# Thresholded attention and max-out FFN on one core: two unscaled quads, 41 half tiles masked by GpSimd, product and out tiles evacuated by VectorE, a new order

## The chip, the cores and the metric

The kernel runs on one core of one Trainium2 chip. The metric is the device time of one execution in microseconds (us). Engines are named as in the profile: PE is TensorE (PEld its weight loads), DVE is VectorE, ACT is ScalarE, POOL is GpSimd, SP is SyncE, which here only issues DMAs.

## The reference

```python
def _attn_ref(q, k, v, tau):                 # (8, 8, 576, 64) each, tau 0.02
    scale = 1.0 / np.sqrt(q.shape[-1])
    scores = scale * np.matmul(q, k.transpose(0, 1, 3, 2))
    thresh = np.max(scores, axis=-1, keepdims=True) - tau
    scores = np.where(scores >= thresh, scores, -1000000000.0)
    scores = scores - np.max(scores, axis=-1, keepdims=True)
    attn = np.exp(scores)
    attn = attn / (np.sum(attn, axis=-1, keepdims=True) + 1e-09)
    return np.matmul(attn, v)

def _moe_ref(x, w1, w2, w3, w_out):          # x (4608, 512), d_ff 768
    h = np.maximum(np.maximum(x @ w1, x @ w2), x @ w3)
    return h @ w_out
```

The heads of the attention's output are put side by side (8 heads of 64 make 512 columns), and the 4608 rows go through the FFN.

## The kernel before, in words

**Tiles.** A quad is four heads of one batch; there are 16 quads (`g`), two a batch. The 576 rows of a head are nine chunks of 64, and a tile joins 128 query rows, so that a quad has nine steps (`idx` 0 to 8), each with two half tiles (`r` 0 and 1) of 128 rows by 576 keys: 16 x 9 x 2 = 288 half tiles. Step 4 joins rows of two heads.

**Path of a half tile.** `transposed` (line 293, letter T) turns q and k on PE; `evacuated` copies them out (a: q by ACT, c: k mostly by DVE); `swapped` (q) copies q to the other 64 partitions, nearly always on POOL. `scores` (324, S) multiplies in float32 into one of four PSUM slots. `maximum` (364, m) lets DVE write minus the scores to a z buffer in SBUF (or the scores less tau) and take the row extremum `nm`. What follows hangs on the half tile's digit in `MASKED` (line 24):

- 0: `threshold` (375, s) makes `th` on DVE; `exponents` (379, e) runs a Prelu on ACT that is flat where the score reaches the threshold; `numerators` (388, n) runs the exponential on ACT, which steeply sends all else to zero and sums the row.
- 2: the same, but Prelu reads the scores in PSUM and needs no s.
- 1: e is the exponential on ACT, and `numerators` (k) masks on DVE: one pass that compares with exp(-tau), multiplies and sums, with both inputs in SBUF.
- 3: as 1, but e reads the scores in PSUM.

Then `reciprocals` (396, r, DVE) inverts the two row sums of a step, `normalized` (400, p, POOL) scales each half of z into the bf16 tile P, and `turned` (409, t) issues one DMA transpose of P on SP's queue into `ptq`.

**Product and FFN.** When the nine steps of a quad are turned, `product` (415, O) multiplies with v: 20 matmuls for each r, of 512 and of 64 columns. The result is copied to `xt` in bf16 by DVE for r = 0 (w) and by ACT for r = 1 (x). When both quads of a batch are there, `ffn` (479) makes 18 hidden pieces (6 slices by 3 weights; F issues the first half of the matmuls, B the second), with ACT copying the first weight's result to `hm` (h) and DVE taking the maximum with the other two (v). The out pieces (also F and B, with `done` at 545) are copied to `ob` by ACT (u) and stored (o) by SP; the last piece is copied by DVE (f) and stored by ACT's queue (d). Row chunk 8 has its own piece (N, j, i). The last batch is split in two parts (`SPLIT`), to shorten the end.

**Order.** Every engine runs its instructions in the order of issue: `_Ordered` (84) chains each to the one before it on its engine. The order is the string `ORDER` (40), written out in the kernel: each letter issues the next instruction of its kind (`issue`, 719), and for S, T, O, F and N a digit names the PSUM slot. Further letters: l loads q, k and v by SP's queue, y casts v on POOL, g loads and z casts weights (POOL).

Of the kernel before, what the change touches and what calls it, by code (L numbers as in the profile page):

```python
# [15 lines left out]
OP = AluOpType  # L16
# [19 lines left out]
PBUFS = 6  # L36

SPLIT = {7: ((0, 1), (2, 3, 4))}

ORDER = """  # L40
lllllllllT0laqqlcT1aS2lcqqgmS0S3lemS1lmnT2lmeS3lsaS0mnqlqemT3lyerclcapsnS1lS2eqmlS3qemznmS2perS1mnpsmnpT3ske
ytS1erkpT2agmnT3pclesqS2aqetS0meqlrnspmS1eqsT2nmpS3tnrcS0zlemS2eprmS3npmtS0npsgS1sermpS2emyS3eptmT0eplmS1ayl
meS0kynS2tssT3snkynkercperlT3pmnpmntqremS0lasprgeT3pmeS2psstnplnS0mzecesqrmS3etqkeS2gpnmS1npsmtnS0prmleS3pmS
2npsmnS0yrsmetperS2epmO1eqtnkplemnzswT2teS3rplS1empnmS3tpnssrS1klepS0mapermtS2epmT1S3nmqtnkO2qemncpS3txrskT1
peS2rmeS0ptmegpamS2npS1ertsmpnlkzS2elmS3eS0mpnlO1srkepsmnO2tyeprgwnpmT1xS3cpeS0sszmF2eS1meBqkF0ngqT3shrsmBay
S2tvpnF3rpemS1BpemF0pnsvT2BnyctS1esrlsT2mphS3lezS1maF0myntpT2sS3ngrcqF1eBmpnS2svpBnrmS3peS0tmeyF2zmnF3lBsvep
S0rhkBptesF2mgeS1zvF0nsmBpteBsrgvpnF1kS3phS2semBnqmF0S3evqF2ntrmBpelS1spvBnlmS3qhF0rsmepS1tnBpsmS3ezvS2eS1rm
pF0etsyO3mnlkngpO2eswetkBxrmpT3nF2rvpaS1BnqmS0hspS3meF2prS1smntBzesmF3ezvT0tBeclT1yS2pnvS0apsmtS3eyrmlS1epS2
mepF0mnqsmnS3tkBnkeF1restpkumeS2prtBumlperkpS0ustS2umS3pesmS1eqtT0mO2nlpceqsrmO3ntywelkS0pxlS1meF3prnS2smBye
myF0thpskS1oeBpF2nlvF3nlrmBpeBkpS1hstsvS0eF3lrmpnF2mBepBsveF1nT0vBtarkS3lhqS2smleF0prF1mnBysntBveS2plvnS0pom  # L50
F3nyS1pmeBsysmF0thT2rrlpeS1clF3epsmBnqT2svBaS1evqS2nmF0pS3nmqBtnmT2pS1hrcpS3esmS0petF2melS1rmpBnF3skpetF0sve
# [53 lines left out]
def kernel(  # L105
# [79 lines left out]

    def load(g, first=False):
        b, qd = quads[g]
        L = Ls[g] = dict(b=b, qd=qd, first=first)

        for n in "qk":  # L190
            L[n] = ld.tile([128, 16, D], F32, name=n + "m")
# [638 lines left out]
```

## Time and profile before

| | before |
|---|---|
| median of 3 runs | 442.02 us (441.42 to 442.81) |
| span of the profiled execution | 440.2 us |
| PE busy | 418.9 us (95%) |
| ACT busy | 403.6 us (92%) |
| DVE busy | 393.9 us (89%) |
| POOL busy | 317.0 us (72%) |
| score matmul records / ph matmuls | 1280 / 2160 |

The span runs from the first to the last instruction; the runs' times lie around it and are a little longer. A row of a group of instructions reads: line, engine, operation, out<-in by the program's names, shapes, count | busy us, mean ns of one | idle time of the engine before them and what ended it. All rows carry line 93, that of the helper that records the order, so tiles are told apart by name: sc is a score tile, z (or stage, when a spare weight buffer serves as z) the working half tile, P the normalized one, ptq the turned one, o the product, ph the hidden and po the out piece in PSUM. A row of windows reads: the stretch, its length, then busy us and (in brackets) instructions of PE, PEld, DVE, ACT and POOL, the granted clock, the share of DMA and GB/s.

### The profile page before, as it was taken

What the parts mean: (1) busy time and instruction counts of PE and PEld (TensorE: products, weight loads), DVE (VectorE), ACT (ScalarE), POOL (GpSimd) and SP (SyncE); (2) the same over time, 40 slices, a digit from 0 to 9 for tenths busy, and PEclk for the clock granted to TensorE, in tenths of its full rate; (3) what the DMA queues carried; (4) which work ended last, traced back from release to release, by engine and by line L of the source; (5) the groups of instructions that cost most, each with busy time, mean ns of one, the idle gap of its engine ahead of it and who ended that gap; (6) DMA issues with size and microseconds to landing.
All of it is one profiled execution on the core that took longest, in us unless ns stands there. A gap on an engine that the chain in (4) does not pass through costs nothing.

```text
span 440.2 us, 14283 instructions
## 1 busy us (share of the span) xinstructions
PE 418.9 (95%) x5188; PEld 313.6 (71%) x5190; DVE 393.9 (89%) x1248; ACT 403.6 (92%) x834; POOL 317.0 (72%) x420
## 2 busy tenths in 40 slices
PE   7696789999999999999999999999999999999996
PEld 6353446787788776787678777887688777786873
DVE  4888899999999999999999999999889999998542
ACT  4999999999999999999999999999999998989521
POOL 1988999998787778867786778886585776554400
PEclk9987999999999999999999999999999999999999
DMA  6999999999999999999999999999698778583812
GB/s 190 276 239 214 270 215 260 263 252 252 220 277 224 237 165 242 291 160 232 189 242 238 202 182 273 192 199 208 135 237 153 147 109 185 102 169 72 192 50 85
DMA packets 213959, 88.50 MB, mean 201 GB/s; under 512 B 189184, under 2 KB 202240, under 8 KB 213888
## 3 DMA queue, kind: packets, MB, share of 16 engines
q1 hardware_dynamic: 213360, 86.96, 95.4%
q8 instruction: 41, 0.67, 0.6%
q10 hardware_dynamic: 528, 0.62, 0.5%
q14 instruction: 30, 0.25, 0.2%
HBM read 35.65 MB, written 9.44 MB: 102 GB/s over the span
## 4 chain that ended last, share of the span: by engine, by line
PE 78%; DVE 5%; POOL 5%; issue 4%; ACT 3%; DMA 2%; SPq 1%; DVEq 0%; POOLq 0%; ACTq 0%
PE ph L93 31%; PE sc L93 26%; PE po L93 10%; PE o L93 8%; POOL P L93 4%; PE tp L93 3%; ACT z L93 3%; DVE z L93 3%; DMA qm<-in_q_dram 2%; SPq L93 1%; DVE kt L93 1%; POOL w L93 1%; DVE stage L93 0%; DVE hm L93 0%; POOL qs L93 0%
## 5 line engine op out<-in xcount | busy, mean ns | idle before, releaser
L93 POOL TENSOR_SCALAR P<-z,rs 128x576 bf16<-128x576 f32 x250 | 202.0, 819 | 59.1 <-DVE rs L93 30.4
L93 DVE TENSOR_SCALAR_CACHE_REDUCE z<-sc 128x576 f32<-128x576 f32 x250 | 183.2, 749 | 12.2 <-PE sc L93 8.1
L93 PE MATMUL sc<-kt,qs 64*128 64x256 f32 (+2 forms) x640 | 179.8, 417 | 5.5 <-DVE z L93 3.9
L93 PE MATMUL sc<-kt,qt 64*128 64x320 f32 (+2 forms) x640 | 180.9, 429 | 3.1 <-DVE z L93 1.2
L93 PE MATMUL ph<-xt,w 64*128 64x288 bf16 (+2 forms) x2160 | 172.0, 283 | 0.2 <-DVE hm L93 0.2
L93 PEld LDWEIGHTS <-w 64*128 64x128 bf16 (+1 forms) x2160 | 128.0, 94 | 31.6 <-issue 4.0
L93 ACT ACTIVATE z<-z,th 128x576 f32<-128x576 f32 x161 | 120.5, 767 | 2.2 <-DVE th L93 1.9
L93 ACT ACTIVATE z<-z 128x576 f32<-128x576 f32 x175 | 117.6, 674 | 0.2
L93 PEld LDWEIGHTS sc<-kt,qs 64*128 64x128 f32 (+1 forms) x640 | 92.4, 179 | 22.5 <-DVE z L93 8.6
L93 PEld LDWEIGHTS sc<-kt,qt 64*128 64x128 f32 (+1 forms) x640 | 92.0, 179 | 14.7 <-DVE z L93 3.5
L93 DVE SCALAR_TENSOR_TENSOR z<-z 128x576 f32<-128x576 f32 x75 | 61.7, 827 | 1.4 <-ACT z L93 1.1
L93 POOL COPY qs<-qt 64x640 f32<-64x640 f32 (+3 forms) x66 | 45.9, 695 | 19.5 <-ACT qt L93 16.1
L93 ACT ACTIVATE z<-z,nm 128x576 f32<-128x576 f32 x72 | 53.9, 767 | 0.0
L93 PE MATMUL po<-wo,hT 64*128 64x512 bf16 (+3 forms) x454 | 53.3, 354 | 0.3
L93 DVE TENSOR_TENSOR hm<-ph,hm 128x576 bf16<-128x576 f32 (+2 forms) x54 | 37.0, 685 | 9.8 <-PE ph L93 9.6
L93 ACT ACTIVATE hm<-ph 128x576 bf16<-128x576 f32 (+2 forms) x54 | 31.9, 590 | 14.3 <-PE ph L93 13.8
L93 PEld LDWEIGHTS <-hT 64*128 64x128 bf16 (+2 forms) x456 | 28.4, 95 | 18.5 <-issue 2.6
L93 DVE TENSOR_TENSOR hT<-ph,hm 128x576 bf16<-128x576 f32 (+2 forms) x54 | 36.9, 683 | 2.8 <-PE ph L93 1.0
L93 PE MATMUL o<-ptq,vb 128*64 128x512 bf16 (+2 forms) x544 | 38.7, 282 | 0.2 <-DVE z L93 0.2
L93 POOL TENSOR_SCALAR P<-stage,rs 128x576 bf16<-128x576 f32 x38 | 29.5, 783 | 11.7 <-DVE rs L93 8.4
L93 ACT ACTIVATION_READ_ACCUMULATOR z<-z 128x1 f32 x175 | 33.6, 192 | 0.0
L93 PEld LDWEIGHTS <-vb 128*64 128x64 bf16 x544 | 22.4, 111 | 14.0 <-issue 5.6
(44 smaller groups left out, 412.2 us busy)
## 6 DMA issues: line engine op xcount, KB each, us to landing
vm<-in_v_dram SPq DMA_DIRECT2D x32, 256.0 KB, 4.6
qm<-in_q_dram SPq DMA_DIRECT2D x15, 512.0 KB, 4.7
km<-in_k_dram SPq DMA_DIRECT2D x15, 512.0 KB, 5.4
out_dram<-ob SPq DMA_DIRECT2D x14, 512.0 KB, 4.5
stage<-in_moe_w_dram SPq DMA_DIRECT2D x9, 512.0 KB, 5.6
ptq<-P SPq DMA_TRANSPOSE x144, 4.5
vr<-in_v_dram SPq DMA_DIRECT2D x16, 128.0 KB, 3.8
stage<-in_moe_w_out_dram SPq DMA_DIRECT2D x3, 512.0 KB, 5.5
```

What stands on the lines that cost most here:

```text
L93: ins = fn(*a, **kw)
```

## The change

**Unscaled quads.** For the quads 0 and 1 (`LOOSE = 2`: batch 0) numerators go straight to P in bf16 without a row sum; r and p fall away. The row sums come from PE: four further products (one for each quad and r) take a column of ones in place of v, broadcast to 64 columns. ACT takes their logarithm (L) into an `ob` buffer and then the exponential of its negative (E), which is one over the sum; when the real product is there, DVE multiplies the two (w). The table set with logarithm and exponential is loaded by name at the start.

**Digits 4 and 5.** For digit 4 (41 half tiles) POOL masks: b adds the threshold to z, multiplies by 2^100 and writes the result as saturated int8 into every second byte of a bf16 tile `far` (a score under the threshold leaves a huge number, any other one zero), C adds `far` to z, and G is ACT's one exponential. Digit 5 is digit 3 with the comparison made on the scores in PSUM against `th`. By digits the 288 half tiles go from 187 / 84 / 14 / 3 (digits 0 to 3) to 192 / 37 / 10 / 2 / 41 / 6 (digits 0 to 5).

**Evacuation.** All products go to DVE (w; no x is left), and the second of each pair of out tiles does too (f: 15 instead of 1, u: 17 instead of 31). Each out pair has its own `ob` tile, `hm` has two buffers instead of three.

**Order.** The string is new throughout. ONE_S, ONE_R and BY_DMA, which would join thresholds or reciprocals of two half tiles or let DMAs do the swaps, are set beyond the range in use and do nothing here. Of the two strings the first seven lines are shown; the diff is cut to its core.

```diff
 FLAT = 2.0 ** -100
 
 MASKED = """
-220202110002002100110000100020020312000112012010100000000010100000001100
-001000111010000101100000000000110001100000011110110200100000100010000000
-110001101110100100010000001001100100000100101111102300000100100000001000
-001000110100100001000000000100100001011110100011011100002100001000001013
+421201000404010544201014040421043014041450550100100000010000000000100001
+000000100050001400100010400000000140000000410000001422400000010000000044
+000040401002210000004000400004000000041000040010101000001004004000010000
+004000000100400100400004401000000400010000105104200040400004001040041032
 """
...
-SPLIT = {7: ((0, 1), (2, 3, 4))}
+FARS = 1
+ONE_S = 999
+ONE_R = 999
+LOOSE = 2
+X_ON_DVE = True
+U_ON_DVE = True
+BY_DMA = 99
+FAR = 2.0 ** 100
+SPLIT = {7: ((0, 1), (2, 3, 4),)}
 ORDER = """
-lllllllllT0laqqlcT1aS2lcqqgmS0S3lemS1lmnT2lmeS3lsaS0mnqlqemT3lyerclcapsnS1lS2eqmlS3qemznmS2perS1mnpsmnpT3ske
-ytS1erkpT2agmnT3pclesqS2aqetS0meqlrnspmS1eqsT2nmpS3tnrcS0zlemS2eprmS3npmtS0npsgS1sermpS2emyS3eptmT0eplmS1ayl
-meS0kynS2tssT3snkynkercperlT3pmnpmntqremS0lasprgeT3pmeS2psstnplnS0mzecesqrmS3etqkeS2gpnmS1npsmtnS0prmleS3pmS
-2npsmnS0yrsmetperS2epmO1eqtnkplemnzswT2teS3rplS1empnmS3tpnssrS1klepS0mapermtS2epmT1S3nmqtnkO2qemncpS3txrskT1
-peS2rmeS0ptmegpamS2npS1ertsmpnlkzS2elmS3eS0mpnlO1srkepsmnO2tyeprgwnpmT1xS3cpeS0sszmF2eS1meBqkF0ngqT3shrsmBay
-S2tvpnF3rpemS1BpemF0pnsvT2BnyctS1esrlsT2mphS3lezS1maF0myntpT2sS3ngrcqF1eBmpnS2svpBnrmS3peS0tmeyF2zmnF3lBsvep
-S0rhkBptesF2mgeS1zvF0nsmBpteBsrgvpnF1kS3phS2semBnqmF0S3evqF2ntrmBpelS1spvBnlmS3qhF0rsmepS1tnBpsmS3ezvS2eS1rm
...
+lllllllllT0laclqqT1S0alqqclmS1lS3mS2lS0melsmeS3blT1mnlCaclS0esmlqeS2mqlGT1ysS0mlalecqmtnqsykS1eyS3nmS2essS0m
+bnS1mnT3CsestmakS0eqT3T2cGlqasmS3tbnmS1eqS2mtnqsemCemT1T0tssS2cabsGS0mqeS1tmqekS0nClS2mnlmS1gysmT0etmT2Gbsnk
+S1CascS3etS2mbnS0kGyT1semCtemS3nmyS2qlessS0mbelsketCmGS3meS2tbmnS0cnCS3tGssmO1eymlGmS0lbLskegS1qntmeCmS0nS3s
+skS1ebS2metGmCS0nmT3ezsmaskyGO3smetbEkO1CngswtkLT3qcES2btS0GmS1eCmO3esrmzGtS1ewpnskgT3palrmS2plsrT1mepS3lezs
+mlnkpgesclS0qeS2rtkpnS3mnO1ymeprsmS0qeS2rspLmO3ezskEtO0pnmelpS2snwgS1qLmlO3yemtEsrysS0npwS2epmtS1eF3ympnBspF
+0mnBzhsT1evF3tS2akS0nrrF1mpetBpmeS2BprnvtS0pnmF3hqsrT2sgBeczF1evS2qgnsmBlepF3mtnpBssvS2pheT0mpS3aF1trspmnS2T
+0znBmS3ecpF2termF0pnBvplS3nsvqS1gesBmzeS2mhF3grnsS1smplS0nmqBleS2symtF1esrF0vpeBknpBveO3pmhtesS1rwpnS2mF0pel
...
 """
...
+                if i == 0 and LOOSE:
+                    scalar.preload_act_table_set("natural_log_exp_and_others")
...
+    def loose(g):
+
+        return g < LOOSE
+
     def masked(g, idx, r):
-        return by_mask[2 * number[g, idx] + r] in "13"
+        return by_mask[2 * number[g, idx] + r] in "135"
+
+    def on_pool(c, r):
+        return by_mask[2 * number[c["g"], c["idx"]] + r] == "4"
...
     def direct(c, r):
 
-        return by_mask[2 * number[c["g"], c["idx"]] + r] in "23"
+        return by_mask[2 * number[c["g"], c["idx"]] + r] in "235"
...
     def maximum(c, r):
 
         z = c["z", r] = half_of_z()
-        nm = c["nm", r] = small.tile([128, 1], F32, name="nm")
+        if r == 0:
+            c["nms"] = small.tile([128, 2], F32, name="nm")
+        nm = c["nm", r] = c["nms"][:, r:r + 1]
...
     def threshold(c, r):
-        th = c["th", r] = small.tile([128, 1], F32, name="th", bufs=5)
-        vector.tensor_scalar(out=th, in0=c["nm", r], scalar1=-1.0, scalar2=tau, op0=OP.mult, op1=OP.subtract)
+        if "ths" not in c:
+            c["ths"] = small.tile([128, 2], F32, name="th", bufs=5)
+        mine = slice(0, 2) if together(c) else slice(r, r + 1)
+        for x in range(mine.start, mine.stop):
+            c["th", x] = c["ths"][:, x:x + 1]
+        vector.tensor_scalar(out=c["ths"][:, mine], in0=c["nms"][:, mine], scalar1=-1.0, scalar2=tau, op0=OP.mult, op1=OP.subtract)
+
+    def limited(c, r):
+
+        return by_mask[2 * number[c["g"], c["idx"]] + r] in "045"
...
     def exponents(c, r):
         z = c["z", r]
         src, sign = (c[r], -1.0) if direct(c, r) else (z, 1.0)
+        if on_pool(c, r):
+            if loose(c["g"]):
+                scalar.activation(out=part_of(c, r), in_=z, func=AF.Exp, bias=c["nm", r], scale=-1.0)
+            else:
+                scalar.activation(out=z, in_=z, func=AF.Exp, bias=c["nm", r], scale=-1.0, accum_out=summed(c)[:, r:r + 1])
+            return
         if masked(c["g"], c["idx"], r):
             scalar.activation(out=z, in_=src, func=AF.Exp, bias=c["nm", r], scale=-sign)
         else:
             th = c["nm", r] if direct(c, r) else c["th", r]
             scalar.activation(out=z, in_=src, func=AF.Prelu, bias=th, scale=sign, alpha=FLAT)
 
+    far = [one.tile([128, S], BF16, name=f"far{x}") for x in range(FARS)]
+    fars = iter(range(1 << 20))
+
+    def marked(c, r):
+
+        c["far", r] = t = far[next(fars) % FARS]
+        pool.tensor_scalar(out=t.bitcast(mybir.dt.int8).rearrange("p (n x) -> p n x", x=2)[:, :, 1],
+                           in0=c["z", r], scalar1=c["th", r], scalar2=FAR, op0=OP.add, op1=OP.mult)
+
+    def moved(c, r):
+        pool.tensor_tensor(out=c["z", r], in0=c["z", r], in1=c["far", r], op=OP.add)
...
+    def part_of(c, r):
+
+        if "P" not in c:
+            c["P"] = pp.tile([128, W], BF16, name="P")
+        return c["P"][:, r * S:(r + 1) * S]
...
     def numerators(c, r):
-        z, acc = c["z", r], c["sm"][:, r:r + 1]
-        if masked(c["g"], c["idx"], r):
-            vector.scalar_tensor_tensor(out=z, in0=z, scalar=thr, in1=z,
+        z = c["z", r]
+        dst, acc = (part_of(c, r), None) if loose(c["g"]) else (z, summed(c)[:, r:r + 1])
+        if by_mask[2 * number[c["g"], c["idx"]] + r] == "5":
+            vector.scalar_tensor_tensor(out=dst, in0=c[r], scalar=c["th", r], in1=z,
+                                        op0=OP.is_ge, op1=OP.mult, accum_out=acc)
+        elif masked(c["g"], c["idx"], r):
+            vector.scalar_tensor_tensor(out=dst, in0=z, scalar=thr, in1=z,
                                         op0=OP.is_ge, op1=OP.mult, accum_out=acc)
         else:
-            scalar.activation(out=z, in_=z, func=AF.Exp, scale=-1.0 / FLAT, accum_out=acc)
+            scalar.activation(out=dst, in_=z, func=AF.Exp, scale=-1.0 / FLAT, accum_out=acc)
...
     def normalized(c):
         c["P"] = P = pp.tile([128, W], BF16, name="P")
         for n in range(2):
             pool.tensor_scalar(out=P[:, n * S:(n + 1) * S], in0=c["z", n],
                                     scalar1=c["rs"][:, n:n + 1], scalar2=1.0, op0=OP.mult, op1=OP.mult)
-            if n:
-                line["t"].append(c)
             yield
...
+    if LOOSE:
+        ones = one.tile([128, 4], BF16, name="ones")
+
+    def product(L, r, target, part=None, sums=False):
+
+        pt = L["pt"]
+        if not sums:
+            vb, vrb = L["vb"], L["vrb"]
...
             for m, (*q0, p0, n) in order:
                 for i in range(2):
-                    w = vb[:, 2 * r + i, (1, 3, 0, 2)[m], :] if m < 4 else vrb[:, 2 * r + i, :]
+                    if sums:
+                        col = 2 if m < 4 else r
+                        w = ones[:, col:col + 1].broadcast_to([128, D])
+                    else:
+                        w = vb[:, 2 * r + i, (1, 3, 0, 2)[m], :] if m < 4 else vrb[:, 2 * r + i, :]
                     tensor.matmul(ps[64 * i:64 * i + 64, p0:p0 + n], w,
                                   pt[:, 4 if m == 4 else m + 5 * r, q0[i]:q0[i] + n],
                                   start=(m == 0), stop=(m == 4))
...
+        def logs():
+            L["inv", r, part] = hp_.tile([128, 2, DM], F32, name="ob").rearrange("p a m -> p (a m)")
+            scalar.activation(out=L["inv", r, part][:, 0:hi - lo], in_=st["ps"][:, base:base + hi - lo], func=AF.Ln)
+
+        def inverses():
+            t = L["inv", r, part][:, 0:hi - lo]
+            scalar.activation(out=t, in_=t, func=AF.Exp, scale=-1.0)
+
+        def scaled():
+            dst = target(L["b"])[:, 2 * L["qd"] + r, :]
+            vector.tensor_tensor(out=dst[:, lo:hi], in0=st["ps"][:, base:base + hi - lo], in1=L["inv", r, part][:, 0:hi - lo], op=OP.mult)
+
+        if loose(L["g"]):
+            p.evacs = [("L", logs), ("E", inverses)] if sums else [("w", scaled)]
+        else:
+            p.evacs = [("w", on_vector) if r == 0 or X_ON_DVE else ("x", on_scalar)]
...
             def done():
                 if wi == 0:
-                    st["hm", f] = hp_.tile([128, nr, n], BF16, name="hm", bufs=3)
...
             def done(a):
-                if a == 0 and (part is None or c % 2 == 0):
-                    st["ob"] = hp_.tile([128, 2, DM], F32, name="ob")
-                both = st["ob"]
+                mine = my if part is None else st
+                if "ob" not in mine or part is not None and c % 2 == 0:
+                    mine["ob"] = hp_.tile([128, 2, DM], F32, name="ob")
+                both = mine["ob"]
...
-                scalar.activation(out=ob, in_=src, func=AF.Copy)
+                if U_ON_DVE and a == 1:
+                    vector.tensor_copy(out=ob, in_=src)
+                else:
+                    scalar.activation(out=ob, in_=src, func=AF.Copy)
...
-            p.kind = "f" if last else "u"
+            p.kind = "f" if last else "uf" if U_ON_DVE else "u"
...
+    for t in far:
+        vector.memset(t, 0.0)
+    if LOOSE:
+        vector.memset(ones, 1.0)
+        for x in range(2):
+            vector.memset(ones[64 - 64 * x:128 - 64 * x, x:x + 1], 0.0)
...
                     for r in range(2):
+                        if loose(g):
+                            yield product(Ls[g], r, x_of, part, True)
                         yield product(Ls[g], r, x_of, part)
...
+    rs = (made[n] for n in range(len(steps)) if n + 1 not in second and not loose(steps[n][0]))
+    ts = (made[n] for n in range(len(steps)))
...
+            for k, fn in p.evacs:
+                line[k].append(fn)
...
         elif what == "m":
             c, r = line["m"].pop(0)
             maximum(c, r)
-            line["e"].append((c, r))
-            if not masked(c["g"], c["idx"], r) and not direct(c, r):
+            if not on_pool(c, r):
+                line["e"].append((c, r))
+            if limited(c, r) and not (together(c) and r == 0):
                 line["s"].append((c, r))
         elif what == "s":
-            threshold(*line["s"].pop(0))
+            c, r = line["s"].pop(0)
+            threshold(c, r)
+            for x in range(2) if together(c) else (r,):
+                if on_pool(c, x):
+                    line["b"].append((c, x))
+        elif what == "G":
+            exponents(*line["G"].pop(0))
+        elif what == "b":
+            c, r = line["b"].pop(0)
+            marked(c, r)
+            line["C"].append((c, r))
+        elif what == "C":
+            c, r = line["C"].pop(0)
+            moved(c, r)
+            line["G"].append((c, r))
...
```

More of the change, by code (lines that the diff above doesn't have):

```diff
@@ L641 @@
     number = {x: n for n, x in enumerate(steps)}
+    second = set()
+    for n in range(max(ONE_R, 0) + 1, len(steps)):
+        (g0, i0), (g1, i1) = steps[n - 1:n + 1]
+        if g0 == g1 and i0 != 4 and i1 != 4 and n - 1 not in second:
+            second.add(n)
     Ls, xts, stores, stores9, ends, ninths = {}, {}, [], [], [], []
```

109 lines of the change are left out of this document (61 added, 48 removed).

## The prediction

> **What bounds the kernel now.** I read the page first, then the table of windows, then the same table for the score tiles alone, and last the timeline for what one instruction occupies.
>
> ```profile
> span 440.2 us, 14283 instructions
> PE 418.9 (95%) x5188; PEld 313.6 (71%) x5190; DVE 393.9 (89%) x1248; ACT 403.6 (92%) x834; POOL 317.0 (72%) x420
> PE   7696789999999999999999999999999999999996
> DVE  4888899999999999999999999999889999998542
> ACT  4999999999999999999999999999999998989521
> POOL 1988999998787778867786778886585776554400
> PE 78%; DVE 5%; POOL 5%; issue 4%; ACT 3%; DMA 2%; SPq 1%; DVEq 0%; POOLq 0%; ACTq 0%
> ```
>
> Four engines are nearly full, but not at the same time. PE is below nine tenths only in the first slices and the last one; there ACT already shows nine. So the early stretch and the rest have different limits. I cut at one place of the order string, the 73rd S (the first score tile of the fifth quad): letters can be counted up to it in both kernels.
>
> ```profile
> 0.00:96.80 96.80, 52.07 (x322) 27.51 (x324) 52.41 (x143) 8.74 (x12) 0.95 1.11 240
> ```
>
> This is the window row of the score tiles (PE, weight loads, DVE, ACT). Seventy-two half tiles make 320 matmul records (four each, eight where idx is 4); 322 have begun, so the 73rd half tile starts at 96.8 us. Cut there, the whole trace gives (length, then PE, weight loads, DVE, ACT, POOL busy):
>
> ```profile
> 6.00:96.80 90.80, 75.48 (x796) 49.68 (x798) 81.39 (x271) 87.83 (x187) 80.94 (x107) 0.94 1.15 249
> 96.80:402.60 305.80, 305.40 (x4020) 236.48 (x4019) 293.72 (x929) 298.51 (x612) 229.00 (x300) 1.00 1.00 201
> 402.60:436.30 33.70, 33.56 (x332) 23.35 (x330) 18.05 (x45) 15.14 (x34) 6.30 (x8) 1.00 0.34 90
> 436.30:440.20 3.90, 0.00 (x0) 0.00 (x0) 0.00 (x0) 0.38 (x1) 0.00 (x0) 1.00 0.45 149
> ```
>
> Up to 96.8 us ACT is the limit: 87.83 of 90.8 us (96.7%), PE 83%. After it PE is: 305.40 of 305.8 and 33.56 of 33.7 us, then 3.9 us of last evacuation and store. So what the change takes off ACT, DVE or POOL is worth time before 96.8 us and hardly any after it. There the time is PE's work.
>
> **What one instruction occupies.** Means overlap their successors, so I go by starts.
>
> ```profile
> 205.47 0.76 ACT L93 ACTIVATE z<-z,nm 128x576 f32<-128x576 f32 x1
> 206.13 0.67 ACT L93 ACTIVATE z<-z 128x576 f32<-128x576 f32 x1
> 206.71 0.19 ACT L93 ACTIVATION_READ_ACCUMULATOR z<-z 128x1 f32 x1
> 206.80 0.77 ACT L93 ACTIVATE z<-z,nm 128x576 f32<-128x576 f32 x1
> ```
> ```profile
> 205.85 0.21 DVE L93 TENSOR_SCALAR th<-nm 128x1 f32<-128x1 f32 x2
> 205.97 0.75 DVE L93 TENSOR_SCALAR_CACHE_REDUCE z<-sc 128x576 f32<-128x576 f32 x1
> 206.64 0.85 DVE L93 SCALAR_TENSOR_TENSOR z<-z 128x576 f32<-128x576 f32 x1
> 207.43 0.75 DVE L93 TENSOR_TENSOR hm<-ph,hm 128x576 bf16<-128x576 f32 x1
> ```
>
> On ACT an exponential with a bias takes 0.66 us, the plain one 0.58 and reading its sum 0.09; letter n is thus 0.67. On DVE the maximum (m) takes 0.67, the mask (k) 0.79, a tiny threshold 0.06; I take 0.08 for a reciprocal. The others come from groups:
>
> ```profile
> L93 POOL TENSOR_SCALAR P<-z,rs 128x576 bf16<-128x576 f32 x250 | 202.0, 819 | 59.1 <-DVE rs L93 30.4
> L93 POOL CAST vb<-vm 128x1024 bf16<-128x1024 f32 x16 | 17.4, 1086 | 3.2 <-PE o L93 2.8
> L93 DVE CAST xt<-o 128x576 bf16<-128x576 f32 (+2 forms) x18 | 12.3, 681 | 3.2 <-PE o L93 3.2
> L93 ACT ACTIVATE xt<-o 128x576 bf16<-128x576 f32 (+2 forms) x18 | 10.5, 591 | 3.2 <-PE o L93 3.2
> L93 ACT ACTIVATE ob<-po 128x512 f32<-128x512 f32 (+1 forms) x36 | 19.6, 581 | 5.7 <-PE po L93 5.6
> L93 DVE COPY ob<-po 128x512 f32<-128x512 f32 x1 | 0.7, 692 | 3.3 <-PE po L93 3.3
> ```
>
> **The first stretch, part by part.** Up to the 73rd S the letters T, a, c, q, y, l and t are equal in both orders, and so are the exponentials (67 against 55 e and 12 G). What differs:
>
> ACT: n falls from 51 to 38 (-13 x 0.67 = -8.7 us). Seventeen of the 38 belong to the unscaled quads and read no sum (-17 x 0.09 = -1.5). The two x are gone (-1.2), h falls from 5 to 4 (-0.6, priced as xt). New are four logarithms and four exponentials for the row sums; no row has them, the nearest are xt from PSUM (0.59) and the biased exponential (0.66): 8 x 0.59 = 4.7, at most 5.3. Sum -7.3: 87.83 becomes 80.5 us.
>
> DVE: m -1 (-0.7), s +9 (+0.5), k +1 (+0.8), r -18 (-1.4), w +2 (+1.4), v -2 (-1.4, priced as xt), memsets some +0.3. Sum -0.5: 80.9 us.
>
> POOL: p falls from 64 to 27 (-37 x 0.819 = -30.3), one weight cast fewer (-1.1), and twelve half tiles get b and C. The b pass has one input as P has, but writes single bytes, which no row shows: from P's 0.82 to the cast's 1.09, and I take P, which has the same 576 elements. The C pass reads 2 x 576 elements; its bounds are one P (0.82) and two (1.64), and the nearest row by elements read is the 1024-wide cast: 1.086 x 1152 / 1024 = 1.22. So 12 x 2.04 = 24.5. Sum -6.9: 74.0 us.
>
> ```profile
> 205.73 1.18 PE L93 MATMUL o<-ptq,vb 128*64 128x512 bf16 x16
> 206.74 0.41 PE L93 MATMUL o<-ptq,vr 128*64 128x512 bf16 x4
> ```
> ```profile
> 91.55 0.98 PE ph L93 x16
> ```
>
> PE: four sum products are added, each a product's 20 matmuls (205.73 to 207.15: 1.42 us), 5.7 us. F and B fall from 14 to 11; a pair is the 16 ph matmuls of this piece of the chain of waits, 0.98 us, so 2.9 us of PE work moves behind the cut. 75.48 becomes 78.3 us.
>
> If ACT keeps its 96.7%, the stretch lasts 80.5 / 0.967 = 83.2 us instead of 90.8. But DVE, with 80.9, would then be at 97%; the most that it holds anywhere in this trace is 293.72 / 305.8 = 96.0%. At 96% it asks for 84.3 us, so the limit changes hands. I take 84.5 (PE at 93%, POOL at 88%): the 73rd S starts at 90.5 us, 6.3 earlier. P without normalization also saves a POOL pass in the latency of each of 18 chunks; DMA transposes in SP's queue keep their number, and loads keep their place among them (l and t are equal at the cut). That latency is in the 96%.
>
> **The rest.** PE's debt is 2.9 us. ACT loses 16 x (-9.4) and 14 u (-8.1), gains 14 n (+9.4) and 29 sums of G (+2.6): 298.5 becomes 293. DVE loses 43 k (-34.0), gains 43 s (+2.6), 16 w (+10.9) and 14 out tiles (14 x 0.69 = 9.7): 293.7 becomes 283. Both have more room, and PE little to win from it:
>
> ```profile
> PEld sc L93 <- DVE z L93: 12.0, 20, 1.4
> PE sc L93 <- DVE z L93: 5.1, 9, 1.2
> DVE xt L93 <- PE o L93: 3.2, 4, 1.2
> ACT xt L93 <- PE o L93: 3.2, 4, 2.0
> ```
>
> PE waited 5.1 us for DVE's z, part of it ahead of the cut; its weight loads waited more, mostly under running matmuls. I credit 1.5 us. The product evacuations stand in DVE's queue alone now: behind a w that waits for PE stand maxima, and behind those PE's own score tiles. The rows give 6.4 us for eight such waits; DVE's 25 us of room covers them; without it they cost PE up to that. The two hm buffers instead of three and the longer life of a PSUM tile that k reads directly (six tiles) cost nothing as long as the order keeps each F's two v close, as it does. Behind the last S both orders have 42 F and five or four O; four small w in a row instead of alternating cost 0 to 0.5 us, hidden by the ninth's matmuls between.
>
> POOL gets 29 x 2.04 = 59 us: 229.0 becomes 289 of 308.7 (94%).
>
> Sum: 90.5 + 343.4 (96.8 to 440.2) + 2.9 - 1.5 = 435.3 us of span. The median of the runs, 442.0, is 1.8 above the profiled span, so **437.1 us**.
>
> **Two rules of the Trainium skill.**
>
> ```profile
> L93 POOL TENSOR_SCALAR P<-z,rs x250: 734/744/1891, 13.0 to 411.6; 128x576 bf16<-128x576 f32 x125
> L93 DVE SCALAR_TENSOR_TENSOR z<-z x75: 732/755/1428, 17.8 to 407.7; 128x576 f32<-128x576 f32 x75
> ```
>
> P and the mask sometimes take twice their median. The Trainium skill, SBUF — State Buffer, "Who interferes with whom", says that a VectorE instruction with two SBUF inputs and a GpSimd instruction that reads SBUF shut each other out for a whole instruction; these rows agree. By that rule 87 such masks become 39, and P's mean may fall from 819 towards 744 ns, up to 19 us of POOL; I leave that out of the sum. Against the change speaks the Trainium skill, GPSIMD Engine Reference, "When to use GPSIMD": elementwise work with two inputs belongs on VectorE. Per half tile that holds here too (2.04 against 0.79 us), but the window rows show 76.8 us of POOL free and 12.1 of DVE.
>
> **The rivals.** (a) POOL becomes the bound (slower). Its place is 96.8 to 402.6 us, where it rises from 75% to 94%. At ACT's 97.6% (298.51 / 305.8) POOL has 301 us; (301 - 230) / 29 = 2.45 us for b and C together is where it starts to decide, and two P passes for C (0.82 + 1.64 = 2.46) stand just there. With the longest P above, 1.89, for C: 230 + 29 x 2.71 = 308.6 / 0.976 = 316, 7.5 us more, and the 1.5 credited is gone: 444.3 of span, **446 us**. For it: P and the swaps stand behind b and C, and in ACT's queue the other half tiles' e and n, and so PE's score banks, stand behind each G that waits for its C. Against: the median P is 744. Chance 0.12. (b) The early gain is lost on DVE's queue: the w and f waits make maxima late, PE gets score tiles late, and 4 to 5 of the 4.9 us are eaten: **442 us**. For it: DVE at 96%. Chance 0.14. (c) More than forecast: DVE holds 99% early (80.9 / 0.99 = 81.7, 2.8 us less) and PE gains 3 us instead of 1.5 later: 431.0 of span, **433 us**. For it: masks that are shut out less. Chance 0.13. (d) It doesn't do what it says:
>
> ```profile
> L93 ACT ACT_TABLE_LOAD x1 | 1.3, 1283 | 2.8 <-issue 2.8
> ```
>
> If logarithm, exponential and Prelu don't share the preloaded table, four logarithms bring eight loads of 1.28 us to ACT before the cut, 10.3 us: some **447 us**. Chance 0.02; the forecast, 435 to 440, has 0.59.
>
> About 0.3% is what a measurement of this kernel can tell: faster means under 440.7, slower above 443.3. Forecast and (c) are faster, 0.59 + 0.13 = 0.72; (b) is the same, 0.14; (a) and (d) slower, 0.14. The range goes from just under (c), 431, to 443, which leaves out (a), (d) and little below.
>
> **What would show it.** In the changed profile the 73rd S (322 score records) starts near 90.5 us, with DVE and ACT both at 95 to 97% before it; PE stays above 99% busy from there to the tail; the C pass takes 1.1 to 1.4 us; POOL's busy time is some 370 us with less than 819 ns a P; one table load, or two. Wrong would be: the 73rd S not before 95 us; PE idle behind it on DVE's z or ACT's z with POOL at 97%; C above 1.7 us.

## The result and the profile after

The changed kernel takes 453.43 us (median of 4 runs, 451.48 to 453.92), the kernel before 441.72 beside it (441.31 to 442.81): a ratio of 1.0253, with a 95% interval of 1.0228 to 1.0278. It is slower, where 437.1 us were forecast. The profiled execution has a span of 451.7 us (before 440.2).

First the page of the changed kernel: span, engines, and the slices of four engines and of PE's granted clock.

```profile
span 451.7 us, 14419 instructions
PE 430.1 (95%) x5270; PEld 316.6 (70%) x5270; DVE 392.7 (87%) x1225; ACT 396.8 (88%) x826; POOL 359.4 (80%) x466
PE   7787889999989999999999999999999999999996
DVE  5999988899887998989899999999989999998542
ACT  3989989999986999999999999999999998997321
POOL 2889996998885887988999997898889988987100
PEclk9999989999998999999999999999999999999999
```

ACT is busy for 6.8 us less, POOL for 42.4 more, PE for 11.2 more. PE's slices hold an 8 where before has only nines (the twelfth), and the clock falls just behind it. Then the window rows of the changed kernel, the score tiles alone and the whole trace cut at the 73rd S (columns as in the prediction):

```profile
0.00:95.30 95.30, 50.48 (x322) 27.03 (x324) 55.09 (x148) 6.57 (x9) 0.96 1.09 230
```
```profile
6.00:95.30 89.30, 78.00 (x828) 49.40 (x830) 81.41 (x253) 82.16 (x153) 76.10 (x94) 0.96 1.13 238
95.30:414.40 319.10, 314.46 (x4078) 240.57 (x4078) 291.68 (x923) 301.19 (x648) 277.40 (x362) 0.99 1.02 197
414.40:447.80 33.40, 33.20 (x324) 22.54 (x320) 17.67 (x42) 11.74 (x26) 5.22 (x6) 1.00 0.35 92
...
35.00:45.00 10.00, 7.82 (x56) 3.46 (x56) 10.00 (x32) 10.00 (x17) 9.27 (x11) 1.00 1.12 198
45.00:55.00 10.00, 8.34 (x96) 5.60 (x96) 9.84 (x29) 9.75 (x18) 9.39 (x10) 1.00 1.10 246
55.00:65.00 10.00, 7.80 (x72) 4.17 (x68) 9.45 (x35) 9.34 (x20) 9.62 (x12) 0.87 1.13 210
65.00:75.00 10.00, 10.00 (x116) 6.28 (x112) 7.98 (x24) 9.01 (x19) 9.58 (x14) 0.96 1.12 272
```

The 73rd S starts at 95.3 us, 1.5 earlier than before and not 6.3. (Three traces of later runs, with the same letters up to that place, start it at 96.9, 96.9 and 97.8 us, the third quad taking 29.4 to 30.1 us in them: a gain of 1.5 us is within what one trace can tell.) From there to the end the changed kernel needs 356.4 us, before 343.4. By the starts of the score tiles (80 records a quad) the third quad begins at 43.8 us (before 49.1), the fourth at 70.8 (71.8): the two unscaled quads bring 5.3 us, and the third quad, 27.0 us long instead of 22.7, gives most of it back. The limit changes inside the stretch: VectorE and ScalarE are full from 35 to 45 us, and from 65 to 75 us PE is.

The groups of the changed kernel that answer to the priced operations (line 101 is the helper that was line 93):

```profile
L101 POOL TENSOR_TENSOR z<-z,far 128x576 f32<-128x576 f32 x34 | 45.1, 1325 | 1.9
L101 POOL TENSOR_SCALAR far<-z,th 128x576 int8<-128x576 f32 x34 | 25.8, 759 | 8.6 <-DVE th L101 6.2
L101 POOL TENSOR_SCALAR P<-z,rs 128x576 bf16<-128x576 f32 x214 | 164.4, 780 | 26.8 <-DVE rs L101 10.0 <-DVE th L101 3.6 <-ACT z L101 3.2
L101 DVE SCALAR_TENSOR_TENSOR z<-z 128x576 f32<-128x576 f32 x27 | 23.8, 883 | 0.1
L101 ACT ACT_TABLE_LOAD x1 | 1.3, 1283 | 2.8 <-issue 2.8
```

And the largest new wait. On SP's queue the k load of the seventh quad stands behind three P transposes, which wait for P, as P waits in GpSimd's queue behind b, C and casts; before, it was issued 10.9 us earlier. SP's timeline, first of the changed kernel, then of before:

```profile
122.33 0.86 SPq L101 DMA_DIRECT2D qm<-in_q_dram  x1
123.29 8.27 SPq L101 DMA_TRANSPOSE ptq<-P  x3
131.61 0.58 SPq L101 DMA_DIRECT2D km<-in_k_dram  x1
```
```profile
120.10 0.57 SPq L93 DMA_DIRECT2D qm<-in_q_dram  x1
120.73 0.67 SPq L93 DMA_DIRECT2D km<-in_k_dram  x1
121.49 2.16 SPq L93 DMA_TRANSPOSE ptq<-P  x1
```

PE's timeline of the changed kernel where it needs that load, and the windows around it:

```profile
136.44 0.47 PE L101 MATMUL tp<-identf,km 64*128 64x64 f32 x8 [2.94 <-DMA km<-in_k_dram]
```
```profile
133.00:136.50 3.50, 0.56 (x11) 0.26 (x7) 0.94 (x5) 2.01 (x5) 2.56 (x3) 1.00 1.09 242
136.50:138.00 1.50, 1.50 (x30) 1.48 (x32) 0.99 (x3) 0.12 (x1) 0.00 (x0) 0.80 1.27 264
138.00:140.00 2.00, 2.00 (x21) 1.77 (x18) 1.31 (x4) 1.80 (x5) 0.59 (x1) 0.50 1.15 68
140.00:142.00 2.00, 2.00 (x27) 1.64 (x26) 1.24 (x2) 0.64 (x2) 1.50 (x3) 0.80 1.06 218
```

PE stands still for 2.94 us, and then the clock column falls to 0.80 and 0.50 for some 5 us.

### The profile page after: what moved, and what is told of

It reads as the page before. It is cut to its first block, busy times and chain, and to the rows that moved or that the text cites. A ratio compares the mean times of both kernels' runs of the same rounds, so it can differ in the third digit from the quotient of the medians.

```text
span 451.7 us, 14419 instructions
## 1 busy us (share of the span) xinstructions
PE 430.1 (95%) x5270; PEld 316.6 (70%) x5270; DVE 392.7 (87%) x1225; ACT 396.8 (88%) x826; POOL 359.4 (80%) x466
## 3 DMA queue, kind: packets, MB, share of 16 engines
q1 hardware_dynamic: 213360, 86.96, 96.8%
## 4 chain that ended last, share of the span: by engine, by line
PE 82%; ACT 5%; DVE 5%; DMA 3%; issue 3%; POOL 1%; SPq 1%; DVEq 0%; POOLq 0%
PE ph L101 31%; PE sc L101 28%; PE po L101 11%; PE o L101 9%; PE tp L101 3%; DVE z L101 3%; ACT z L101 2%; ACT P L101 2%; DMA ptq<-P 1%; DMA km<-in_k_dram 1%; SPq L101 1%; DMA qm<-in_q_dram 1%; ACT qt L101 1%; POOL P L101 0%; DVE ob L101 0%
## 5 line engine op out<-in xcount | busy, mean ns | idle before, releaser
L101 POOL TENSOR_SCALAR P<-z,rs 128x576 bf16<-128x576 f32 x214 | 164.4, 780 | 26.8 <-DVE rs L101 10.0
L101 ACT ACTIVATE z<-z,th 128x576 f32<-128x576 f32 x167 | 124.4, 767 | 5.4 <-DVE th L101 5.0
L101 ACT ACTIVATE z<-z 128x576 f32<-128x576 f32 x159 | 106.9, 674 | 0.3
L101 PEld LDWEIGHTS sc<-kt,qt 64*128 64x128 f32 (+1 forms) x640 | 91.8, 177 | 17.8 <-DVE z L101 8.1
L101 POOL COPY qs<-qt 64x640 f32<-64x640 f32 (+3 forms) x66 | 43.9, 665 | 10.9 <-ACT qt L101 7.3
L101 POOL TENSOR_TENSOR z<-z,far 128x576 f32<-128x576 f32 x34 | 45.1, 1325 | 1.9
L101 ACT ACTIVATE z<-z,nm 128x576 f32<-128x576 f32 x57 | 43.7, 766 | 1.0 <-POOL z L101 0.9
L101 PEld LDWEIGHTS <-vb 128*64 128x64 bf16 x544 | 20.8, 111 | 17.9 <-issue 8.3
L101 DVE TENSOR_SCALAR th<-nm 128x1 f32<-128x1 f32 x239 | 32.4, 146 | 1.0
```

What stands on the lines that cost most here:

```text
L101: ins = fn(*a, **kw)
```

## The experiments

Theory 1: the parts are worth what was priced, and the loss sits in the new order, above all in that late load. Theory 2: the parts themselves cost it (evacuations in VectorE's queue, marks on GpSimd, row sums on PE). Theory 3 is rival (a), GpSimd as the bound. Every time is a median, with before at 441.6 to 442.0 us beside it. Changes of the order string are shown as the letters around them.

**The late load alone.** One letter l moves ahead of three t. (The load is the seventh quad's; the expectation names the sixth, in whose time PE needs it.)

```
-srpslS2ufS1ptnmT3S0pecS2termO3pnmnO1smtbeswCeS0wlS3mt
+srpsllS2ufS1ptnmT3S0pecS2termO3pnmnO1smtbeswCeS0wS3mt
```


> The changed kernel with one letter moved: the load of k of the sixth quad (the 48th l) is issued right behind the l before it, ahead of the three P transposes that it stood behind on SP's queue. Theory 1 (the loss sits in the new order, and the largest piece is this load: it is issued at 131.6 us, lands 4.7 us later, PE waits 2.9 us for it, and then runs 5 us at a granted clock of 0.5 to 0.8): 4 to 6 us less than the changed kernel, 447.5 to 449.5 us, no wait of PE for km over 0.5 us, no clock under 0.9 between 133 and 142 us. Theory 2 (the parts themselves cost the time: the half tiles masked on POOL, the evacuations on VectorE, the sum products on PE) and theory 3 (POOL is the bound behind the cut): within 1.5 us of the changed kernel, 452 to 455 us, because what is won at 136 us is lost again to the next engine that is behind.

451.05 us (450.19 to 452.63), ratio to before 1.0203 (1.0179 to 1.0227): half of what was expected. The window of this run where the wait was:

```profile
133.00:136.50 3.50, 3.50 (x62) 3.01 (x60) 3.46 (x12) 3.48 (x8) 3.23 (x5) 1.00 1.01 209
136.50:138.00 1.50, 1.50 (x29) 1.27 (x27) 1.50 (x4) 1.50 (x5) 0.92 (x1) 1.00 1.91 114
138.00:140.00 2.00, 2.00 (x34) 1.22 (x30) 2.00 (x9) 2.00 (x5) 1.72 (x2) 1.00 0.78 166
```

PE is full and the clock stays at 1.00. From the 73rd S (96.9 us here) to the end the traced execution needs 351.9 us, 4.5 less than the changed kernel; its 73rd S, with the same letters ahead of it, came 1.6 us later in this trace, so less of it shows in the time.

**Head and end apart.** The orders are cut at the 73rd S and put together crosswise, with the marks and evacuations that belong to each half.

```
-ORDER, MASKED: the changed kernel's
+ORDER, MASKED: the changed kernel's up to the 73rd S, before's from there on
-X_ON_DVE, U_ON_DVE = True, True
+X_ON_DVE, U_ON_DVE = False, False
```


> The changed kernel's order, marks and unscaled quads up to the 73rd S, from there on the kernel before: its order, its marks, and every second product and all out tiles on ScalarE. Work that before does ahead of the 73rd S and the changed kernel behind it comes first. Theory 1 (the head of the change is worth its 1.5 us, the loss of 13.0 us lies in the order behind the cut): before's 440.2 us of span less 1.5, plus 2.9 for the three F tiles that the head leaves over: 441.6 us of span, 443.4 us. Theory 2 (the debt of the head keeps costing further on, as full queues and late transfers): 446 to 452 us.

446.57 us, ratio 1.0100 (1.0077 to 1.0123). With the F tiles that the new head leaves over put first, the 73rd S starts at 99.7 us, before at 96.8 with the same work done; from there the old end takes 344.4 us, 1.0 more than before. So the new head is not 3.4 us faster net of its debt, as the forecast had it, but 2.9 slower: without the debt of 2.9 it takes as long as the old one. Theory 1 was wrong on the head. The other way round:

```
-ORDER, MASKED: the changed kernel's
+ORDER, MASKED: before's up to the 73rd S, the changed kernel's from there on
-LOOSE = 2
+LOOSE = 0
```


> The other way round: the kernel before up to the 73rd S (no unscaled quads, no marks of 4 there), from there on the changed kernel's order, marks and evacuations. Theory 1 (the loss lies behind the cut, in the order and the late load): the changed kernel's 451.7 us of span, plus 1.5 for the later 73rd S, less 2.9 for the three F tiles that are done already: 450.3 us of span, 452 us, with the wait of PE for km in it. If the loss comes out of the head (a debt, or loads that start late because of it): 440 to 445 us.

453.20 us, but it tells little, because of a window behind the seam:

```profile
101.00:106.00 5.00, 2.63 (x22) 1.36 (x20) 5.00 (x17) 4.63 (x11) 3.42 (x5) 0.77 0.81 196
```

PE is busy for 2.63 of 5 us. Neither kernel waits there; the run measures its seam too.

**Are the row sums the price?** Four times 20 matmuls become four times 4; the rest of the row sums is left out.

```
                 for i in range(2):
+                    if sums and m:
+                        continue
...
-func=AF.Ln)
+func=AF.Ln, bias=1.0)
```


> The changed kernel with the four row sum products cut from 20 matmuls to 4 (the rest of the row sums is left out, and Ln adds 1 so that it stays finite); all instructions of the other engines remain. Theory 1 (from about 65 us on PE sets the pace, and the sum products are late work of PE): four times 1.1 us, 4 to 5 us less than the changed kernel, 448.5 to 449.5 us, the 73rd S near 91 us. Theory 2 in the form that VectorE and not PE holds the third and fourth quad: within 1 us of the changed kernel, the 73rd S still at 94 to 95.5 us.

451.97 us: 1.5 less than the changed kernel, with runs that overlap (449.88 to 453.17 us, the changed kernel's 451.48 to 453.92). The same cut in the run with the early load, and in the new head with the old end:

> The new order with the early k load (451.05 us) and the short row sums (most of the row sums is left out). The short sums alone gave 1.5 us, beside a k load that stayed late (PE waited 2.2 us for it). If the sums are PE work that counts in full once that load is early: 446 to 447.5 us. If not: 449 to 451 us.

> The new head with the old end (446.57 us), its four row sum products cut from 20 matmuls to 4 (most of the row sums is left out, Ln adds 1). If the sums' 5 us of PE work are what the head costs: 442 to 443 us, level with the kernel before. If the loads and P buffers of the third quad hold it: 445 to 447 us.

450.48 us (0.6 less) and 446.45 us (0.1 less). About 5 us of PE work are gone and the time hardly moves. PE's longest waits say what takes its place: its score tiles wait for VectorE. First the changed kernel, then with short sums:

```profile
PE sc L101 <- DVE z L101: 5.4, 9, 1.7
```
```profile
PE sc L101 <- DVE z L101: 8.5, 14, 1.7
```

With the early load the same wait grows from 5.4 to 8.1 us. And another chain is about as long. The chain of waits from 40 to 98 us, first of the changed kernel, then of the new head with the old end, both with full sums and, but for the F tiles put in at its end, with the same letters up to the 73rd S:

```profile
by line: PE sc L101 36.1%; PE ph L101 23.4%; DVE z L101 14.2%; PE o L101 12.9%; issue 8.5%; PE tp L101 2.5%; DVE th L101 1.4%; DVE xt L101 1.2%; DVE P L101 0.4%; DVEq L101 0.1%
```
```profile
by line: issue 19.0%; POOL P L101 16.8%; DVE z L101 14.4%; PE sc L101 13.3%; DMA qm<-in_q_dram 9.2%; POOL w L101 7.0%; POOL qs L101 4.8%; PE o L101 4.7%; PE ph L101 4.1%; POOL z L101 3.0%; SPq L101 2.9%; POOL far L101 2.6%; POOL vr L101 1.4
```

In the first trace the chain that ends last is PE's and VectorE's. In the second it is largely GpSimd's, with P, its casts and copies, and a q load.

**The loads and transposes of the third quad.** The fourth quad's q and k loads go ahead of three t (and in a second run with short sums); then the q load ahead of one t.

```
-S2tbmnS0cnCS3tGssmO1eymlGmS0lbLs
+S2tbmnS0cnCS3tGssmO1eymGmS0bLs
...
-mbelsketCmGS3me
+mbelllsketCmGS3me
```


> The run with the early k load, and beside it the q and k loads of the fourth quad moved ahead of the three P transposes that they stand behind on SP's queue (in that run's trace q was issued at 44.5 us, PE waited 2.0 us for it at 49.5 us and then had a granted clock of 0.50 from 50 to 55 us). Theory 1 (a load that stands behind transposes costs its wait and a slow clock after it): 1 to 3 us less than with the one early load, 448 to 450 us, and no granted clock under 0.9 between 45 and 60 us. Theory 2 (the third quad is held by VectorE's passes, and PE waits there in any case): within 0.7 us of the 451.05 us with one early load.

454.36 us: 3.3 more than with the one early load, where less was expected. VectorE's waits and the windows of this run:

```profile
DVE P L101 <- DMA ptq<-P: 5.9, 1, 5.9
```
```profile
48.00:52.00 4.00, 0.00 (x0) 0.00 (x0) 0.01 (x1) 2.56 (x4) 1.49 (x3) 0.88 1.22 181
52.00:56.00 4.00, 1.97 (x14) 1.63 (x15) 4.00 (x12) 1.98 (x4) 0.89 (x2) 0.50 1.11 255
```

Here is a wait that the change makes possible. In the unscaled quads a VectorE mask or a ScalarE exponential writes P itself, so with the transposes late it is VectorE that stands still for a free P tile, 5.9 us, and with it PE. Before, only GpSimd wrote P.

> The same, with the four row sum products cut from 20 matmuls to 4 (most of the row sums is left out, Ln adds 1). Theory 1 (PE is the limit from the third quad to the end, so its added work counts in full once no late load eats it): 4 to 5 us less than with both early loads alone, 443.5 to 446 us. Theory 2 (VectorE and ScalarE hold the first four quads, PE has room for the sums there): 0.5 to 1.5 us less, as the short sums alone gave.

451.06 us, 3.3 less than the same with full sums.

```
-nCS3tGssmO1eymlGm
+nCS3ltGssmO1eymGm
```


> The new order with the early k load (451.05 us), and the q load of the fourth quad moved ahead of one of the three transposes that it stands behind, not of all three (all three, with the k load beside it, gave 454.4 us: VectorE waited 5.9 us for a P buffer). If the q load's lateness (2.0 us wait, then a granted clock of 0.50) is worth something and one transpose may come 0.7 us later: 448 to 450 us. If the transposes give back what the load wins: 450.5 to 454 us.

450.89 us: nothing won or lost.

**VectorE's masks in the third quad.** Six marks 1 and 5 become 0.

```
-O3smetbEkO1CngswtkLT3qc
+O3smetbEnO1CngswtnLT3qc
...
-mS3lezsmlnkpgescl
+mS3lsezsmlnnpgescl
```

> The run with the early k load, and in it the six half tiles of the third quad that VectorE masks (1.0 to 1.25 us each) are masked on ScalarE (one pass of 0.72 us more each). If VectorE sets the time of the third quad (it is busy 10.00 of 10 us from 35 to 45 us and 9.84 of 10 from 45 to 55 us in the changed kernel): 2 to 5 us less, 446 to 449 us, the third quad 24 to 26 us long in place of 27.1 to 29.4. If the late q load or PE sets it: 450 to 452 us.

450.99 us, as with the early load alone. The chain of waits from 40 to 98 us now runs over ScalarE's z for 28.1%, where that of the run with the early load holds none: VectorE got room, and ScalarE, with six more passes, takes its place.

**PE's clock.** Matmuls that nothing reads are put into two waits of PE, in the run with the early load.

```
+        if (L["g"], idx, r) in ((2, 2, 1), (2, 5, 1)):
+            for _ in range(7):
+                tensor.matmul(ps[:, 0:128], identf, identf, start=True, stop=True)
         return ps[:, first:first + S]
```


> The new order with the early k load (451.05 us), with seven matmuls of 128x128 that nothing reads behind the 42nd and the 48th score tile, where PE then waits 1.96 and 1.71 us in that run's trace (into unused columns of the same tile, about 1.5 us each). If the slow clock behind the waits takes the gain (0.50 from 50 to 55 us: some 2.5 us of PE): no clock under 0.9 between 48 and 66 us, 447 to 449 us. If the other engines' queues set the time of the third quad: clock up, time within 1 us of 451.05.

450.38 us, 0.7 less. The row from 50 to 55 us of the run with the early load, then of the run with fillers:

```profile
50.00:55.00 5.00, 4.21 (x36) 2.57 (x36) 2.70 (x8) 3.23 (x6) 4.67 (x5) 0.50 1.22 248
```
```profile
50.00:55.00 5.00, 3.99 (x63) 2.83 (x61) 3.85 (x11) 4.47 (x8) 4.57 (x6) 1.00 1.22 216
```

The clock stays up, and PE gets ahead: it turns k at 60.11 us, in the run with the early load at 62.19. But the second filler takes most of that back. It stands in the score tile that VectorE reads next, so VectorE waits for its end, and PE then waits for VectorE as long as without it (1.71 us; the helper is line 102 here):

```profile
63.05 0.76 DVE L102 TENSOR_SCALAR_CACHE_REDUCE z<-sc 128x576 f32<-128x576 f32 x1 [1.79 <-PE sc L102]
```
```profile
64.61 0.48 PE L102 MATMUL sc<-kt,qs 64*128 64x256 f32 x1 [1.69 <-DVE z L102]
```

So the run does not show what the slow clock costs. In the old order:

```
+            if (L["b"], L["qd"], n, r) == (1, 0, "k", 0):
+                for _ in range(9):
+                    tensor.matmul(ps[:, 384:512], identf, identf, start=True, stop=True)
```


> The kernel before, in the text of the changed one (441.57 us), with nine such matmuls behind the transposes of k of the third quad, where PE waits 2.5 us for VectorE and the clock is 0.50 from 40 to 45 us. ScalarE is 5.00 of 5 us busy there: if it sets the stretch, the clock goes up and the time stays, 441 to 442.2 us. If the slow clock has a price there too: 439 to 440.5 us, faster than both kernels.

443.30 us, 1.7 above the control below; the clock still fell to 0.50 from 40 to 45 us. Neither reading had that. Here too the filler stands in VectorE's way: the copy of k waits 0.58 us for its end and starts at 35.78 us, in the control at 35.16. The rest is left open, and so is the price of the clock.

**The parts in the new order, behind the cut.** In the run with the early load, first the evacuations, then the marks 4 go back to ScalarE.

```
-            p.evacs = [("w", on_vector) if r == 0 or X_ON_DVE else ("x", on_scalar)]
+            p.evacs = [("w", on_vector) if r == 0 or X_ON_DVE and L["g"] < 4 else ("x", on_scalar)]
-U_ON_DVE = True
+U_ON_DVE = False
```


> The run with the early k load (451.05 us), and in it every evacuation that the change gives to VectorE from the fifth quad on is back on ScalarE at the same place of the order: the second product of each quad and every second out tile, 28 of some 0.7 us. Theory 1 (behind the cut PE is the limit; in the new order the evacuations on VectorE cost nothing): no gain, 450.5 to 454 us. Theory 2 (VectorE's added evacuations hold PE up behind the cut): 447 to 449.5 us.

```
 (MASKED, the 29 marks 4 from the fifth quad on)
-4 (letters b, C, G)
+0 (letter e at the place of b, n at the place of G)
```


> The run with the early k load, and in it the 29 half tiles from the fifth quad on that GpSimd masks are masked on ScalarE as the unmarked ones are (one more ScalarE pass each, two GpSimd passes less, with the ScalarE passes at the places of the GpSimd ones). Theory 1: GpSimd (about 2.1 us each, 61 us less) was never the limit, ScalarE takes 21 us more over 350 us: no gain, 451 to 456 us. Theory 3 (GpSimd's queue behind the cut holds P, the transposes and the loads, and through them PE): 445 to 449 us.

457.31 and 458.74 us, 6.3 and 7.7 more. In this order both parts are worth their place; so behind the cut theories 2 and 3 are wrong.

**The parts in the old order.** First all evacuations on VectorE:

```
-X_ON_DVE, U_ON_DVE = False, False
+X_ON_DVE, U_ON_DVE = True, True
```


> The kernel before in its order and with its marks, P scaled everywhere; only the evacuations are moved as in the change: all attention products and every second out tile of a pair on VectorE. Theory 1 (the parts as such are nearly free where PE is the limit): 440.5 to 443 us, within 1.5 us of the kernel before. Theory 2 (the evacuations load VectorE, on which PE waits for score tiles): 444 us or more, with more PE waits for z of VectorE than 6.4 us in all.

456.91 us, ratio 1.0335 (1.0314 to 1.0356). With the old marks VectorE keeps 87 masks beside the new evacuations (the changed kernel leaves it 45). One window of this run shows it full (28.97 of 29 us), with ScalarE at 24.75:

```profile
254.00:283.00 29.00, 28.13 (x344) 19.26 (x342) 28.97 (x88) 24.75 (x49) 22.06 (x27) 1.00 0.95 214
```

Then a little of the change in the first four quads, and the same without the three marks; and as a control the kernel before in the new text.

```
-gS1sermpS2emyS3eptmT0eplmS1aylmeS0kynS2tssT3snk
+bCgS1sermpS2myS3eptmT0eplmS1aylmeS0kynS2tssT3sGk
...
-LOOSE, X_ON_DVE, U_ON_DVE = 2, True, True
+LOOSE, X_ON_DVE, U_ON_DVE = 0, True, False
...
-("w", on_vector) if r == 0 or X_ON_DVE else
+("w", on_vector) if r == 0 or X_ON_DVE and L["g"] < 4 else
```


> The kernel before in its order, with a little of the change and only where ScalarE is the limit (up to the 73rd S): the evacuations of the first four quads' products on VectorE, and three half tiles of the first, third and third quad marked 4 (pass and add on GpSimd, one ScalarE pass less each). No row sum products, and everything from the fifth quad on as before. ScalarE is relieved of four evacuations of 0.7 us, two to three of them ahead of the 73rd S, and three passes of 0.73 us, some 4 us. If ScalarE sets the pace there and PE takes the time up: the 73rd S 2 to 3.5 us earlier than 96.8 us, 438.5 to 440 us. If GpSimd (89% busy there, 6.1 us more) or VectorE sets it instead: 441.5 to 444 us.

> The run of the old order with the small relief of ScalarE in the first four quads, without its three half tiles on GpSimd: only the second product of each of the first four quads is evacuated by VectorE, all else is the kernel before. If the 8.8 us that that run lost came from the three half tiles on GpSimd (VectorE waited 7.5 us for z buffers that GpSimd held, against 2.8 us before): 440.5 to 443 us. If they came from the evacuations in VectorE's queue: 446 to 450 us.

```
-LOOSE, X_ON_DVE, U_ON_DVE = 2, True, True
+LOOSE, X_ON_DVE, U_ON_DVE = 0, False, False
```


> The order, marks, scaling and evacuations of the kernel before, in the text of the changed kernel (one more memset for the far tile, and small tiles shared by two halves). All theories: 441.5 to 442.5 us; 443 us would say that the 1.6 us of the run with the head's evacuations are the text's and not the evacuations'.

450.48, 443.31 and 441.57 us. The control equals the kernel before. Three marks on GpSimd cost 7.2 us in an order that was not made for them, four evacuations 1.7. VectorE's waits for z tiles that P still holds, of before and of the run with the marks:

```profile
DVE z L93 <- POOL P L93: 3.0, 8, 0.8
```
```profile
DVE z L101 <- POOL P L101: 7.5, 9, 2.1
```

Without the marks, with the evacuations alone, it is 1.6 us. Two more passes on GpSimd make the P behind them late, and P keeps its z tile. No run beat the kernel before.

## Why the prediction was wrong, step by step

**The sums of busy time held within 3%.** Up to the 73rd S 80.5 (ACT), 80.9 (DVE), 74.0 (POOL) and 78.3 us (PE) were forecast; the row of the changed kernel has 82.16, 81.41, 76.10 and 78.00.

**The step that failed first: "At 96% it asks for 84.3 us, so the limit changes hands. I take 84.5".** Measured: 89.3 us (90.9 to 91.8 in the three later traces with the same letters), with ACT at 92%, DVE at 91%, PE at 87%, POOL at 85%. A share that one engine reached in a stretch of one limit was lent to a stretch in which the limit moves (ACT and DVE to about 45 us, then DVE, then PE), and no engine is full in all of it. The experiments took candidates away one at a time: row sums, six VectorE masks, the q load's place. None of them, taken out of the order as it stood, gave back more than 1.5 us, and the fillers that kept the clock up cost time themselves. What is shown is that work taken off one engine comes back as a wait for another: with short sums PE waits longer for VectorE's z, with six masks off VectorE the chain runs over ScalarE's z, with loads ahead of transposes VectorE waits for P tiles. That points to several chains of nearly equal length. How much each of them holds, and how the third quad would have to be ordered, was not found.

**The second: "loads keep their place among them (l and t are equal at the cut)".** Equal counts at one place say nothing of the order before and behind it. This k load is the 48th l, and in both orders it stands behind the 91st S; but before, no t stands between it and the q load, and now there are three. It came 10.9 us later than before, PE waited 2.94 us, and moving that one letter shortens what follows the 73rd S by 4.5 us in the traces and the time by 2.4.

**The rest.** 343.4 + 2.9 - 1.5 = 344.8 us were forecast behind the cut, 356.4 came: 2.9 debt as forecast, 4.5 of the late load, 1.0 by which the old end too is longer behind the new head (344.4), and 4.6 left over (351.9 - 344.4 - 2.9). The last stands in no wait; PE's waits from 97 to 388 us in the run with the early load, all of them, come to 1.1 us:

```profile
PE o L101 <- DVE hm L101: 0.5, 1, 0.5
PE po L101 <- DVE ob L101: 0.4, 1, 0.4
PE sc L101 <- DVE ob L101: 0.2, 1, 0.2
```

Counted from each matmul's start to the next one's, most of it lies in PE's own work: the 960 score matmuls behind the 73rd S take 112.6 us in that run and 110.6 in the new head with the old end, the ph matmuls 135.4 (1984 of them) and 130.5 (1936). Why they follow each other more slowly stays open. The credit of 1.5 us for fewer waits did not come.

**The rivals.** (a) GpSimd did not become the bound: C takes 1.325 us (estimate 1.22, the rival's price 1.64), b 0.759, POOL is busy for 359.4 us (some 370), and taking 29 marks off it costs time. (b) came nearest to what happened early, a gain that is lost, but at 442 us and by VectorE's queue alone; the loss went on behind the cut. (c) Nothing of its gain came. (d) There is one table load. Only (a) and (d) had the sign right, at 446 and 447 us, and neither mechanism occurred.

**The two rules.** P's mean fell from 819 to 780 ns with fewer masks, and the remaining masks' (on z) rose from 827 to 883 ns, beside GpSimd passes that read two inputs. No run takes the two apart. The Trainium skill, SBUF — State Buffer, "Who interferes with whom", fits both; the prediction bounded the saving at 75 ns a pass, and about half of that came. The Trainium skill, GPSIMD Engine Reference, "When to use GPSIMD", would have had the masks on VectorE; that was not tried in the new order.

## What to carry to other kernels

Busy time summed over a stretch forecasts its length only where one engine is the limit in all of it: cut at every change of the limit, and ask of each cut which chain stands right behind the one that is removed. When an order is rewritten, compare every load's issue with its first use, not letter counts: one load behind three transposes cost 2.4 us of the time. A part that pays in an order planned for it can cost in another: evacuations on VectorE were worth 6 us in the new order (from the fifth quad on) and cost 15 in the old one, where VectorE also keeps its 87 masks.

A filler has a price of its own: matmuls put into a wait must not stand in a tile that another engine is about to read.

## What the runs showed of the hardware

The granted clock can fall behind short waits of PE. After one of 2.94 us it was 0.80, 0.50 and 0.80 in the next 5.5 us. In the run with the early load this wait, of PE's timeline, stands ahead of its 0.50 from 50 to 55 us:

```profile
49.52 0.46 PE L101 MATMUL tp<-identf,qm 64*128 64x64 f32 x8 [1.96 <-DMA qm<-in_q_dram]
```

With matmuls that nothing reads in it the clock stayed at 1.00. Not every such wait lowers it: in the same run one of 1.71 us was followed by a clock of 1.00.

```profile
64.95 0.48 PE L101 MATMUL sc<-kt,qs 64*128 64x256 f32 x1 [1.71 <-DVE z L101]
```
```profile
65.00:70.00 5.00, 5.00 (x54) 3.20 (x56) 4.75 (x18) 4.85 (x11) 4.59 (x7) 1.00 1.23 293
```

The Trainium skill, TensorE: Matmul & The Clock Gate, "HAM oscillation — how this bites in real kernels", gives idle gaps over some 3.4 us as the rule of thumb; these rows show the fall behind shorter ones, of 1.96 and 2.94 us.
